# Row maxima of an attention unit: a 32x32 transpose on VectorE, or a transfer in four-byte pieces

## The chip, the cores and the metric

The kernel runs on one core of a Trainium2 chip. Its engines are named as in the profile: PE (TensorE, matmuls; PEld is its weight load), DVE (VectorE), ACT (ScalarE), POOL (GpSimd) and SP (SyncE, which here only issues DMAs). Each works through its own instructions in order and waits for others at semaphores. The metric is the device time of one execution in microseconds (us), the median of several runs.

## The reference

The input `x` has 2048 rows of 512. A scalar gate per row mixes an attention with 32 heads of size 16, which share one key and one value head, and a gated feed-forward layer. All is in float32.

```python
g = sigmoid((x * gate_w).sum(-1, keepdims=True))
q = (x @ wq).reshape(1, 2048, 32, 16).transpose(0, 2, 1, 3)
k, v = x @ wk, x @ wv
p = softmax(einsum("bhqd,bkd->bhqk", q, k) * 16 ** -0.5)
a = einsum("bhqk,bkd->bhqd", p, v).transpose(0, 2, 1, 3).reshape(1, 2048, 512) @ wo
b = ((x @ w_gate) * (x @ w_up)) @ w_down
out = g * a + (1 - g) * b
```

## The kernel before

The attention is cut into 64 units. A unit is 128 query rows of one group of 8 heads; `Q[u]` holds its queries transposed, four heads in each half of the partitions (0 to 63, 64 to 127). A softmax needs the maximum of each row of scores before the exponentials, so each unit is gone through twice.

The first pass (`p1`) makes scores with queries along the partitions: 32 matmuls a unit (L760), each 128 queries by 512 keys, and DVE takes the maximum of each (L761) into `mx`. After the 32nd, `p1_end` makes the unit's final maxima, 128 queries by 8 heads. The second pass (`p2`) makes the scores again, now with keys along the partitions: 32 matmuls (L801), each with an `Exp` on ACT (L802). The negated maximum enters these matmuls as two more rows of `Q`, rows 48 and 49 of each half: a high part in the format float32r, and a low part that holds what the rounding lost. So a unit's second pass can't begin before its two rows are in `Q`. After that `pv` sums the weighted values (L814), and `o_chain` normalises: a store of the sums, loads of them and of the denominators (`raw`, `dn`), sum (L658, L660) on POOL, reciprocals on DVE, a store of these (`dr`, L671), a load that spreads them (`rb`, L675), and a product on POOL (L679).

In `m` a query lies on a partition; in `Q`'s rows the queries lie along the row. Between them stands a transposition. Before the change it is DVE's: L769 takes the last maximum, L772 transposes blocks of 32x32, L773 negates and rounds, and L775 takes the low part. Four small DMAs then store the rows in DRAM (`dm`), one for each block, and two load them into `Q` (L788), one for each half.

Between these matmuls PE works on the feed-forward layer and the projections (L959). All of it is written out by a planner in the kernel: strings of letters set the order of the matmuls, and functions given to `later` are called when a modelled clock comes to them. `spend("dve", 800.0)` tells the planner that DVE is busy for 800 ns. The store is set 300 ns behind that, the fetch 3200 ns behind the store, and `mat[u]` tells when the second pass may start. These times only set places in the order; on the chip semaphores hold each instruction until what it needs is there. The first pass runs some 25 steps ahead of the second (`LEAD`).

All DMAs named here are issued by SP, in the planner's order. An instruction that waits there holds all DMAs behind it. POOL makes in the same way, in order, the splits of weights and hidden values into high and low parts (L142, L143), the products of the feed-forward layer (L581) and sums (L395).

Of the kernel before, what the change touches and what calls it, by code (L numbers as in the profile page):

```python
# [14 lines left out]
F32 = mybir.dt.float32  # L15
F32R = mybir.dt.float32r
AF = mybir.ActivationFunctionType
OP = mybir.AluOpType
AX = mybir.AxisListType
# [54 lines left out]
def mix_kernel(ctx: ExitStack, tc: tile.TileContext, x, wq, wk, wv, wo, wg, wu, wd, gw, out):  # L74
    nc = tc.nc
    PSUM = bass.MemoryType.PSUM
    consts = ctx.enter_context(tc.tile_pool(name="consts", bufs=1))
    work = ctx.enter_context(tc.tile_pool(name="work", bufs=2))
# [30 lines left out]
    z = consts.tile([128, NC * NT], F32, name="z")  # L109
    gg = consts.tile([128, NC * NT], F32, name="gg")  # L110
    gb = consts.tile([128, NC * NT], F32, name="gb")
    mm = [consts.tile([128, 32], F32, name=f"mm{i}") for i in range(2)]
    for t in mm:
        nc.gpsimd.memset(t, 0.0)
    woh = consts.tile([128, 4, D], F32R, name="woh")
    wol = consts.tile([128, 4, D], F32R, name="wol")

# [8 lines left out]
    def later(ns, fn):  # L126
        heapq.heappush(events, (clock["T"] + ns, next(serial), fn))
# [5 lines left out]
    def spend(eng, ns, after=0.0):  # L133
        clock[eng] = max(clock[eng], clock["T"], after) + ns
        return clock[eng]
# [26 lines left out]
    def bank(i, name):  # L162
        return psum.tile([128, 512], F32, name=name, tag=f"bank{i}")

    def ms_bank(i):
        return bank(i, f"ms{i}")
# [582 lines left out]
    mx, mat = {}, {}  # L749

    def p1(k, half, b):
        u, slot, kq = order1[k]
        c, g, t = units[u]
        q = Q[u]
        if u not in mx:
            mx[u] = work.tile([128, 8, 4], F32, name="mx", bufs=2)
            left[u] = 32
        p = bank(b, "s1")
        r = KROWS[half]
        nc.tensor.matmul(p, q[r, slot], KK[r, kq * 512:(kq + 1) * 512], start=True, stop=True)  # L760
        nc.vector.tensor_reduce(mx[u][:, half * 4 + slot, kq:kq + 1], p, axis=AX.X, op=OP.max)  # L761
        left[u] -= 1
        if left[u] == 0:
            p1_end(u)

    def p1_end(u):
        q = Q[u]
        m = mm[u % 2]
        nc.vector.tensor_reduce(m[:, 0:8], mx.pop(u), axis=AX.X, op=OP.max)  # L769
        w = work.tile([128, 3, 32], F32R, name="mt", bufs=2)  # L770
        mt = w[:, 0].bitcast(F32)
        nc.vector.transpose(mt, m)  # L772
        nc.vector.tensor_reduce(w[:, 1], mt.rearrange("p (q v) -> p q v", v=1), axis=AX.X, op=OP.max, negate=True)  # L773
        with nc.allow_low_precision(reason="the low part of two that are kept"):
            nc.vector.tensor_reduce(w[:, 2], w[:, 0:2].bitcast(F32).rearrange("p v q -> p q v"), axis=AX.X, op=OP.add)  # L775
        end = spend("dve", 800.0)
        d = dram.tile([2, 8, 128], F32, name="dm", tag="dm", bufs=2)

        def store():
            for b in range(4):  # L780
                nc.sync.dma_start(d[:, :, b * 32:b * 32 + 32].rearrange("v c q -> c v q"),
                                  w[b * 32:b * 32 + 8, 1:3].bitcast(F32))
            later(3200, fetch)

        def fetch():
            for half in range(2):
                r = half * 64 + 48
                nc.sync.dma_start(q[r:r + 2].bitcast(F32), d[:, half * 4:half * 4 + 4, :])  # L788
            mat[u] = clock["T"] + 4000.0
        later(end - clock["T"] + 300.0, store)  # L790
# [32 lines left out]
    p = bank(6, "warm")  # L823
# [3 lines left out]
    p = bank(6, "gwb")  # L827
# [8 lines left out]
    p = ms_bank(1)  # L836
# [21 lines left out]
    p = ms_bank(0)  # L858
# [234 lines left out]
    while events or front or st["gen"] or st["next"]:  # L1093
        run_events()
        if peek():
            j = take()
            items = j.prods()
            p = j.p
            if p is None:
                p = ms_bank(turn)  # L1100
# [24 lines left out]
```

## Time and profile before

| | |
|---|---|
| three timed runs | 1587.06, 1587.61, 1587.9 us |
| span of the profiled execution | 1586.4 us |
| what lies around the span (median less span) | 1.2 us |
| busy: PE, DVE, ACT, POOL | 1581.4, 1364.3, 1202.5, 732.5 us |
| L761, maxima of the first pass, 2048 times | 685 ns each, 1290.4 us |
| L772, L773, L775, 64 times each | median 211, 186, 222 ns |
| DMA packets, bytes | 184995, 121.20 MB |

The page gives a span and no other time of the profiled execution, so the third row takes the runs' median. Rows of the views read: line of the kernel, engine, operation, output and inputs by the program's names. Rows of a timeline begin with the start and the length in us, several equal instructions merged (x4). Rows of waits give the total in us, how often, and the longest. Rows of windows give the busy time of PE, PEld, DVE, ACT and POOL with the count of instructions in brackets, the granted clock of PE, the share of the DMA engines and GB/s; for one line alone, PE and PEld only.

### The profile page before, as it was taken

The page shows a single profiled execution, that of the slowest core. Times are in us where ns is not written, and L with a number is a line of the kernel's source. Part 1 is how long each engine was busy: PE and PEld are TensorE (multiplying, and loading weights), DVE is VectorE, ACT ScalarE, POOL GpSimd, SP SyncE. Part 2 cuts the span into 40 slices and gives each one's busy share as a digit, 9 for nine tenths or more (in the row PEclk, how much of TensorE's full clock was granted, in tenths as well). Part 3 has the DMA queues.
Part 4 walks back from the last instruction along what each step waited for, and adds up shares of the span by engine and source line. Part 5 has one row for each costly group of instructions (what it writes and reads, how often), then busy time and mean ns, then how long its engine had stood idle before and what let it go on. Part 6 is the DMA issues. An engine that isn't in the chain of part 4 may idle for free.

```text
span 1586.4 us, 35431 instructions
## 1 busy us (share of the span) xinstructions
PE 1581.4 (100%) x13144; PEld 1034.1 (65%) x13144; DVE 1364.3 (86%) x2411; ACT 1202.5 (76%) x2384; POOL 732.5 (46%) x871
## 2 busy tenths in 40 slices
PE   9999999999999999999999999999999999999999
PEld 7775666675665666675665666666666666676675
DVE  6998889898898889898898889898988989898982
ACT  5787787777787787777787787877787786877776
POOL 7535736253633624454532725444442615555340
PEclk9999999999999999999999999999999999999999
DMA  6554322122232212131232212122132212212111
GB/s 196 190 175 119 94 62 74 42 71 57 67 103 79 73 49 74 42 87 54 60 103 72 74 55 74 49 69 65 54 117 65 74 55 74 62 55 59 36 32 42
DMA packets 184995, 121.20 MB, mean 76 GB/s; under 512 B 46198, under 2 KB 154614, under 8 KB 184823
## 3 DMA queue, kind: packets, MB, share of 16 engines
q1 hardware_dynamic: 183620, 118.61, 25.1%
q8 instruction: 104, 1.70, 0.5%
q14 instruction: 69, 0.56, 0.1%
q10 hardware_dynamic: 1202, 0.33, 0.1%
HBM read 82.70 MB, written 36.17 MB: 75 GB/s over the span
## 4 chain that ended last, share of the span: by engine, by line
PE 99%; DVE 1%; issue 0%; POOL 0%; POOLq 0%
PE ms L959 32%; PE acc L814 29%; PE s L760 18%; PE s L801 17%; PE ms L155 1%; PE ms L1049 1%; DVE mx L761 0%; PE px L283 0%; PE wo L155 0%; PE warm L825 0%; PE px L270 0%; PE pv L325 0%; PE pick L725 0%; PE gwb L828 0%; DVE y L736 0%
## 5 line engine op out<-in xcount | busy, mean ns | idle before, releaser
L761 DVE TENSOR_REDUCE mx<-s 128x1 f32<-128x512 f32 x2048 | 1290.4, 685 | 170.0 <-PE s L760 107.7
L802 ACT ACTIVATE P<-s 128x512 f32<-128x512 f32 x2048 | 1056.1, 629 | 259.1 <-PE s L801 207.3
L760 PE MATMUL s<-KK,Q 48*128 48x512 f32 x2048 | 703.3, 401 | 0.2
L801 PE MATMUL s<-Q,KK 50*128 50x512 f32 x2048 | 701.9, 407 | 0.0
L814 PE MATMUL acc<-P,V 128*32 128x512 f32 x4096 | 478.8, 597 | 0.0
L801 PEld LDWEIGHTS s<-Q,KK 50*128 50x128 f32 x2048 | 355.5, 185 | 124.5 <-ACT P L802 47.6
L760 PEld LDWEIGHTS s<-KK,Q 48*128 48x128 f32 x2048 | 355.8, 185 | 101.7 <-issue 51.9
L959 PE MATMUL ms<-xh,wl 64*128 64x512 f32 x896 | 318.1, 392 | 0.0
L959 PE MATMUL ms<-xh,wh 64*128 64x512 f32 x896 | 313.6, 394 | 0.0
L959 PE MATMUL ms<-xl,wh 64*128 64x512 f32 x896 | 302.7, 391 | 0.0
L814 PEld LDWEIGHTS acc<-P,V 128*32 128x32 f32 x4096 | 117.9, 109 | 255.2 <-issue 221.0
L581 POOL TENSOR_TENSOR hf<-gs 128x512 f32<-128x512 f32 x56 | 72.1, 1287 | 216.3 <-ACT gs L570 216.3
L959 PEld LDWEIGHTS ms<-xh,wh 64*128 64x128 f32 x896 | 160.2, 186 | 14.6 <-issue 0.8
L959 PEld LDWEIGHTS ms<-xh,wl 64*128 64x128 f32 x896 | 159.3, 186 | 9.1
L959 PE MATMUL ms<-wdh,hl 64*128 64x512 f32 x448 | 162.1, 393 | 0.0
L679 POOL TENSOR_TENSOR oT<-raw,rb 128x128 f32<-128x128 f32 x63 | 29.0, 460 | 285.4 <-DMA rb<-dr 285.3
L959 PE MATMUL ms<-wdh,hh 64*128 64x512 f32 x448 | 160.3, 392 | 0.0
L959 PEld LDWEIGHTS ms<-xl,wh 64*128 64x128 f32 x896 | 152.2, 186 | 10.6
L395 POOL TENSOR_TENSOR y<-y,yt 128x512 f32<-128x512 f32 x58 | 74.7, 1288 | 171.8 <-ACT yt L394 163.6
L143 POOL TENSOR_TENSOR wl<-wn,wh 128x512 fp32r<-128x512 f32 x116 | 149.2, 1286 | 9.3
L959 PE MATMUL ms<-wdl,hh 64*128 64x512 f32 x448 | 153.3, 392 | 0.0
L818 ACT COPY osb<-acc 128x512 f32<-128x512 f32 x64 | 37.5, 587 | 95.3 <-PE acc L814 88.9
(179 smaller groups left out, 1375.5 us busy)
## 6 DMA issues: line engine op xcount, KB each, us to landing
do<-osb SPq DMA_DIRECT2D x63, 256.0 KB
wn<-in_B_w_gate_dram SPq DMA_DIRECT2D x56, 256.0 KB
wn<-in_B_w_up_dram SPq DMA_DIRECT2D x56, 256.0 KB
wdn<-in_B_w_down_dram SPq DMA_DIRECT2D x56, 256.0 KB
Q<-dq SPq DMA_DIRECT2D x384, 32.0 KB
raw<-do SPq DMA_DIRECT2D x252, 32.0 KB
dq<-oh SPq DMA_DIRECT2D x16, 256.0 KB
dq<-ol SPq DMA_DIRECT2D x16, 256.0 KB
```

The source lines that it names most:

```text
L143: nc.gpsimd.tensor_tensor(lo, src, hi.bitcast(F32), op=OP.subtract)
L155: nc.tensor.matmul(p, l, r, start=start and i == 0, stop=stop and i == len(prods) - 1)
L395: nc.gpsimd.tensor_tensor(y[c, t], y[c, t], tmp, op=OP.add)
L581: nc.gpsimd.tensor_tensor(hf, gu[0], gu[1], op=OP.mult)
L679: nc.gpsimd.tensor_tensor(dst, raw[:, 0], rb, op=OP.mult)
L760: nc.tensor.matmul(p, q[r, slot], KK[r, kq * 512:(kq + 1) * 512], start=True, stop=True)
L761: nc.vector.tensor_reduce(mx[u][:, half * 4 + slot, kq:kq + 1], p, axis=AX.X, op=OP.max)
L801: nc.tensor.matmul(p, KK[r, j * 128:(j + 1) * 128], q[r].rearrange("p s q -> p (s q)"), start=True, stop=True)
L802: nc.scalar.activation(P[s][:, half], p, AF.Exp, scale=0.25)
L814: nc.tensor.matmul(acc[u][b:b + 32, :], V[:, j + i], src[:, half], start=(j == 0), stop=(j == NJ - 2))
L818: nc.scalar.copy(osb, acc.pop(u))
L959: nc.tensor.matmul(j.p, lhs[HALVES[l]], rhs[HALVES[l]], start=(l == 0 and i == 0), stop=(l == 1 and end))
```

## The change

DVE keeps the last maximum (now L767), without the padding to 32 columns. POOL negates and rounds it (`tensor_scalar`, L768) and takes the low part (`tensor_tensor`, L769). Nothing is transposed on an engine: one DMA (L774) writes each of the 2048 numbers to its place in the rows in DRAM, in pieces of four bytes. The fetch is as before. Lines behind the change move up, by 2 to 8.

```diff
-    mm = [consts.tile([128, 32], F32, name=f"mm{i}") for i in range(2)]
-    for t in mm:
-        nc.gpsimd.memset(t, 0.0)
...
     def p1_end(u):
         q = Q[u]
-        m = mm[u % 2]
-        nc.vector.tensor_reduce(m[:, 0:8], mx.pop(u), axis=AX.X, op=OP.max)
-        w = work.tile([128, 3, 32], F32R, name="mt", bufs=2)
-        mt = w[:, 0].bitcast(F32)
-        nc.vector.transpose(mt, m)
-        nc.vector.tensor_reduce(w[:, 1], mt.rearrange("p (q v) -> p q v", v=1), axis=AX.X, op=OP.max, negate=True)
-        with nc.allow_low_precision(reason="the low part of two that are kept"):
-            nc.vector.tensor_reduce(w[:, 2], w[:, 0:2].bitcast(F32).rearrange("p v q -> p q v"), axis=AX.X, op=OP.add)
-        end = spend("dve", 800.0)
+        m = work.tile([128, 8], F32, name="m1", bufs=2)
+        w = work.tile([128, 2, 8], F32R, name="mw", bufs=2)
+        nc.vector.tensor_reduce(m, mx.pop(u), axis=AX.X, op=OP.max)
+        nc.gpsimd.tensor_scalar(w[:, 0], m, -1.0, None, op0=OP.mult)
+        nc.gpsimd.tensor_tensor(w[:, 1], m, w[:, 0].bitcast(F32), op=OP.add)
+        end = spend("pool", 450.0, spend("dve", 260.0) + 100.0)
         d = dram.tile([2, 8, 128], F32, name="dm", tag="dm", bufs=2)
 
         def store():
-            for b in range(4):
-                nc.sync.dma_start(d[:, :, b * 32:b * 32 + 32].rearrange("v c q -> c v q"),
-                                  w[b * 32:b * 32 + 8, 1:3].bitcast(F32))
+            nc.sync.dma_start(d.rearrange("v c q -> q (v c)"), w.bitcast(F32).rearrange("q v c -> q (v c)"))
             later(3200, fetch)
```

The new `spend` also moves the store and the fetch among SP's DMAs, and the two operations take a place among POOL's. The matmuls' and ACT's order stays as it is, but for some 80 places of PE in the first stage.

POOL at the end of unit 12, before the change (`den`, `raw`: sums of `o_chain`; `wh`, `wl`, `wdh`, `wdl`: parts of the weights; `hf`, `hh`, `hl`: the hidden values):

```order
L143 TENSOR_TENSOR wl<-wn,wh 128x512
L658 TENSOR_TENSOR den<-dn 128x8
L660 TENSOR_TENSOR raw<-raw 128x128
L142 CAST wdh<-wdn 128x512
L143 TENSOR_TENSOR wdl<-wdn,wdh 128x512
```

The same place now:

```order
L140 TENSOR_TENSOR wl<-wn,wh 128x512
L655 TENSOR_TENSOR den<-dn 128x8
L657 TENSOR_TENSOR raw<-raw 128x128
L768 TENSOR_SCALAR mw<-m_5425 128x8
L769 TENSOR_TENSOR mw<-m_5425,mw 128x8
L139 CAST wdh<-wdn 128x512
L140 TENSOR_TENSOR wdl<-wdn,wdh 128x512
```

The pair stands behind `raw`, and the splits of the next weights behind the pair.

SP at unit 1, before (`xd`: a store of transposed input for later; `dq`: queries in DRAM; `woh`, `wdl` stand here for parts of that input):

```order
L230 DMA Q<-dq 16x4x128 x6
L781 DMA dm<-mt 8x2x32 x4
L334 DMA xd_526<-wdl 128x512
L214 DMA dq<-oh 128x512
L214 DMA dq<-ol 128x512
L334 DMA xd_527<-woh 128x512
L788 DMA Q<-dm 2x512 x2
```

And now:

```order
L227 DMA Q<-dq 16x4x128 x6
L331 DMA xd_522<-wdl 128x512
L774 DMA dm<-mw 128x16x1
L331 DMA xd_523<-woh 128x512
L211 DMA dq<-oh 128x512
L211 DMA dq<-ol 128x512
L780 DMA Q<-dm 2x512 x2
```

The store of the maxima has gone behind one `xd` store; between it and the fetch stand three DMAs, where there were four.

## The prediction

> **What bounds the kernel now.** I read the page first (engines, chain), then the stages by windows, then the waits of TensorE, then the rows around one unit's end on each engine that the change touches. From the page, busy time by engine and the chain that ended last:
>
> ```profile
> span 1586.4 us, 35431 instructions
> PE 1581.4 (100%) x13144; PEld 1034.1 (65%) x13144; DVE 1364.3 (86%) x2411; ACT 1202.5 (76%) x2384; POOL 732.5 (46%) x871
> PE 99%; DVE 1%; issue 0%; POOL 0%; POOLq 0%
> ```
>
> A busy PE is not yet a PE that loses nothing, so two windows of 10 us, one early and one in the middle, and all that the waits list for PE's matmuls, and for its weight loads on the transposed maxima:
>
> ```profile
> core 0: us, PE busy (x) PEld busy (x) DVE busy (x) ACT busy (x) POOL busy (x), PEclk, DMA share, GB/s
> 50.00:60.00 10.00, 10.00 (x68) 8.34 (x68) 9.88 (x18) 6.62 (x15) 5.40 (x5) 1.00 0.72 257
> 700.00:710.00 10.00, 10.00 (x88) 7.93 (x84) 9.69 (x16) 8.76 (x18) 4.21 (x5) 1.00 0.35 99
> ...
> PE warm L825 <- POOL ident masks.py:199: 1.4, 1, 1.4
> ...
> PEld s L760 <- DVE mt L773: 6.7, 8, 0.8
> ```
>
> PE waits once, before its first matmul. The eight weight loads released by the maxima's reduces run ahead of matmuls that did not wait, so their 6.7 us are no gain to be had. In the middle of the run 88 matmuls go in 10 us at full clock; PE's own stream is the bound there, and DVE, at 9.69 of 10, keeps up. Only early on, at 50 to 60 us, with 68 matmuls and DVE at 9.88, does DVE set the pace. So less work on DVE can gain almost nothing, while anything that makes PE wait costs its full length. The question is whether a unit's maxima still arrive in time.
>
> **What is taken from DVE.** The end of the thirteenth unit (counted from 0, unit 12) on DVE:
>
> ```profile
> 334.18 0.18 DVE L769 TENSOR_REDUCE mm<-mx 128x8 f32<-128x32 f32 x1
> 334.40 0.21 DVE L772 STREAM_TRANSPOSE mt<-mm 128x32 f32<-128x32 f32 x1
> 334.65 0.19 DVE L773 TENSOR_REDUCE mt<-mt 128x32 fp32r<-128x32 f32 x1
> 334.87 0.22 DVE L775 TENSOR_REDUCE mt<-mt 128x32 fp32r<-128x64 f32 x1
> 335.01 2.47 DVE L761 TENSOR_REDUCE mx<-s 128x1 f32<-128x512 f32 x4
> ```
>
> L769 stays. The three behind it go: 0.21 + 0.19 + 0.22 = 0.62 us, 40 us of DVE over 64 units. All of that lies beside a PE that does not wait, so it is worth nothing, but for the first unit's end at 47 us, in the stretch where DVE sets the pace: at most 0.6 us, which I take. The two memsets of `mm` lie in the start, on POOL, ahead of nothing that is waited for: nothing.
>
> **The path of the maxima.** From the end of L769 to the first matmul that reads the result: DVE's rest, four stores, the landing, two fetches, their landing, L801. SP's rows for unit 12, and the count of L801 up to two times (384 is twelve units of 32, so unit 12 starts between them):
>
> ```profile
> 335.12 1.29 SPq L781 DMA_DIRECT2D dm<-mt  x4
> 336.51 0.41 SPq L181 DMA_DIRECT2D wn<-in_B_w_up_dram  x1
> 337.41 0.54 SPq L788 DMA_DIRECT2D Q<-dm  x2
> ...
> 0.00:343.70 343.70, 132.85 (x384) 66.53 (x384) 1.00 0.37 116
> 0.00:343.80 343.80, 132.85 (x385) 66.53 (x385) 1.00 0.37 116
> ```
>
> L769 ends at 334.36 and PE wants the rows at 343.75: 9.4 us. Today the first store follows 0.8 us behind L769, and 2.3 us later the fetch can go; issued by 337.95, it has some 5 us.
>
> **POOL's part.** Two operations on 128x8, priced by the nearest row, the sum of denominators L658 on the same shape, 0.20 us each; with two hand-overs I take 0.5 us from the moment POOL is free. POOL works in order, though. Its rows when L769 ends; the new pair stands behind `raw` and ahead of the cast of `wdh`:
>
> ```profile
> 335.10 1.27 POOL L143 TENSOR_TENSOR wl<-wn,wh 128x512 fp32r<-128x512 f32 x1
> 336.33 0.20 POOL L658 TENSOR_TENSOR den<-dn 128x8 f32<-128x8 f32 x1
> 336.49 0.45 POOL L660 TENSOR_TENSOR raw<-raw 128x128 f32<-128x128 f32 x1
> 336.89 0.61 POOL L142 CAST wdh<-wdn 128x512 fp32r<-128x512 f32 x1
> ```
>
> So POOL comes to the pair at 336.94, 2.6 us after L769. Unit 46 is like it: L769 on DVE, `raw` on POOL, and PE's start of the unit (1472 are 46 units of 32):
>
> ```profile
> 1143.92 0.19 DVE L769 TENSOR_REDUCE mm<-mx 128x8 f32<-128x32 f32 x1
> ...
> 1146.26 0.46 POOL L660 TENSOR_TENSOR raw<-raw 128x128 f32<-128x128 f32 x1
> ...
> 0.00:1153.60 1153.60, 507.10 (x1473) 256.04 (x1473) 1.00 0.28 82
> ```
>
> The same reading at all units, by the place of the pair in the new order: POOL is there within 0.4 us, or waits for L769 itself, in about half; 1.3 to 1.6 us late in about a dozen; 2.6 us late in ten, unit 12 to unit 46; over 3 us late in six, four of which have 11.3 us instead of 9.4. Where POOL comes early, the pair now holds the work behind it until L769 has ended, 5 us at most. That work feeds PE, but the matmuls' only wait names POOL before the start, and a POOL that is busy 46% makes it up: nothing.
>
> **The new store.** One DMA in place of four saves 0.9 us of SP's time and issues 2048 pieces of four bytes, over all 16 DMA engines, in place of 64 of 128 bytes. The nearest row is the store of the reciprocals, 128 pieces of 32 bytes from 128 partitions to DRAM. SP's issue and the load that waits for its landing, then the stretch in which its pieces move, then one on a load of the same count of pieces (`dn`) that goes over two engines only, then the queue's totals:
>
> ```profile
> 626.18 0.35 SPq L671 DMA_DIRECT2D dr<-rc  x1
> 626.57 0.43 SPq L181 DMA_DIRECT2D wn<-in_B_w_gate_dram  x1
> 627.60 0.61 SPq L675 DMA_DIRECT2D rb<-dr  x1
> ...
> 627.00:627.20 0.20, 0.20 (x4) 0.16 (x4) 0.00 (x0) 0.00 (x0) 0.00 (x0) 1.00 0.38 21
> 325.80:326.40 0.60, 0.60 (x8) 0.53 (x6) 0.60 (x1) 0.60 (x2) 0.52 (x2) 1.00 0.11 7
> ...
> q1 hardware_dynamic: 183620, 118.61, 25.1%
> ```
>
> Issue to landing is 1.42 us with 128 pieces, and these move at 21 GB/s, 1.5 ns a piece over all engines. 1920 pieces more at that pace are 3.0 us: landing after 4.4 us. The low end is the other load: 128 pieces in 0.6 us on two engines are 9.4 ns a piece on one engine, and 120 more on each would add 1.1 us: 2.5 us. The high end is the mean packet of the queue, 25.1% of 16 x 1586.4 us over 183620 packets, 34.7 ns: 120 of them add 4.2 us: 5.6 us. I take 4.4, since the row is a store to DRAM spread like the new one, and keep 2.5 and 5.6 for the range. No row has a piece of four bytes, so more than 5.6 isn't excluded either.
>
> The Trainium skill has a rule that speaks against this store: "DMA: Bandwidth & Descriptors", section Bandwidth, gives a floor of about 10.5 ns a packet for small transfers, measured on loads. The row above, at 1.5 ns a piece, does not agree, if the rule is meant for a whole transfer; by it the pieces alone would be an estimated 21.5 us.
>
> **The sum for one unit.** Unit 12: pair done 337.45, store lands 341.85, the fetch, a small DMA like the one that took 1.42 us, lands by 343.3; wanted at 343.75. On time by 0.45 us, where today it has some 4. Unit 46, the last of that class, reads the same (pair 1147.2, landing 1151.6, fetch 1153.0, wanted by 1153.6). Where POOL is free, the pair is done 0.6 us behind L769 and the margin is near 3 us. What is late at 4.4 us stands in the first units, where POOL and SP are in arrears. Unit 1 on SP, where the new store goes behind the `xd` store that now follows it, and the count of L801 (32 is one unit):
>
> ```profile
> 72.03 3.65 SPq L230 DMA_DIRECT2D Q<-dq  x6
> 75.78 1.38 SPq L781 DMA_DIRECT2D dm<-mt  x4
> 77.21 0.34 SPq L334 DMA_DIRECT2D xd<-wdl  x1
> ...
> 0.00:81.40 81.40, 11.02 (x32) 5.46 (x32) 1.00 0.58 196
> 0.00:81.60 81.60, 11.09 (x33) 5.56 (x33) 1.00 0.58 197
> ```
>
> SP is free at 75.7, stores `xd` for 0.35, issues at 76.1; landing 80.5, fetch in at 81.9, wanted at 81.5: 0.4 us late. In unit 0 POOL is the one: its L769 ends at 47.1, but the pair stands behind this multiplication, and PE wants the rows at 56.3:
>
> ```profile
> 49.08 1.29 POOL L342 TENSOR_TENSOR yt<-P,wdn 128x512 f32<-128x512 f32 x1
> ...
> 0.00:56.20 56.20, 0.00 (x0) 0.00 (x0) 1.00 0.53 174
> 0.00:56.40 56.40, 0.08 (x1) 0.08 (x1) 1.00 0.53 174
> ```
>
> Pair done 50.9, landing 55.3, fetch in at 56.7: 0.4 us late. Units 3 and 6 are late by 0.2 and 0.6, read in the same way. Together 1.6 us, and I take 2.0, since DMA is 72% busy in the window shown of that stage; all of it PE waiting. Sum: 1586.4 + 2.0 - 0.6 = 1587.8 us of span. The three timed runs have a median of 1587.61, 1.2 us above this span, so 1589.0 us as it is timed.
>
> SP waits with the fetch for the landing, up to 2 us longer than now, and loads behind the store find 128 pieces ahead of them on each engine. What is late next is the row of reciprocals `rb` and POOL's product with it:
>
> ```profile
> POOL oT L679 <- DMA rb<-dr: 285.3, 53, 12.3
> ```
>
> POOL already idles there for 5.4 us at a time without PE waiting; nothing, as long as it stays at 3 us more.
>
> **Rivals.**
>
> Slow pieces (the other side). Four bytes in DRAM may cost more than 32, and PE then waits for the bias rows. It decides from a landing of about 4.6 us: the ten units like unit 12 are then late together, and every further 0.1 us costs 1 us. At 5.6 us the same reading of all units finds 33 late by 24 us in all: 1611. At 7.2 us, 60 are late, mostly by 1 to 2.5 us: 96 us, 1683. Beyond that each microsecond costs 64. For it speaks that no row shows such a piece; against it that the 32-byte row needs so little.
>
> Cheap pieces: at the low end of 2.5 us no unit is late, and the first unit's 0.6 us remain: 1587. It can't be told from the forecast in the result, only in the profile.
>
> DVE's relief frees PE. If DVE held PE by more than the waits show, 64 x 0.62 us could come back in part; at a tenth, 4 us: 1583. The 88 matmuls a window and the lack of waits speak against it.
>
> A floor for each piece of the whole transfer. If pieces go one behind another at 10.5 ns, landing is 18.5 us later than in my sum, and less the margins of 0.4 to 3 us each unit is late by some 16.5 us: 64 x 16.5 = 1056, near 2640 us. The skill's floor, named above, is the reason to give it a chance at all.
>
> **How the numbers follow.** The timing can tell about 0.2% here, 3.2 us. A landing under 4.6 us, forecast and cheap pieces together: 0.50, all of it within 0.2% but for a little. Slow pieces: 0.42, of it 0.15 up to 1611 and 0.15 between there and 1670. DVE's relief: 0.05. The floor: 0.03. So faster 0.05, same 0.50, slower 0.45. The range leaves out the relief beyond 1585.5 and what lies above 1670; the likeliest case's own is 1586.5 to 1591.
>
> **What would show it.** In the changed profile: L772 to L775 gone and DVE at about 1325 us; POOL about 26 us busier; packets near 312,000, since 131,072 come and 4,096 go; from the new store's issue to the fetch some 4.4 us where the fetch stands right behind it; no wait of PE or PEld for a DMA on Q outside the first units. Wrong would be windows with fewer than 88 matmuls in the middle and a gap ahead of L801 once a unit: then the store is slower than I hold it to be.

## The result, and the profile after

The changed kernel takes 2027.11 us (median of four runs, 2023.06 to 2029.74), against 1587.63 us before. The ratio is 1.276, with a 95% interval of 1.2747 to 1.2777. The forecast was 1589.0 us, and the time lies far above its range of 1585.5 to 1670. Two single executions below, one of 5459.73 us with POOL's part alone and one of 3132.42 us with pieces of 64 bytes, lie far from all others at a full clock, and the ratios are made without them. The profiled execution has a span of 2028.0 us, 441.6 us more than before.

From the page after: busy times, the clock in 40 slices, packets, and the chain that ended last, by engine and by line.

```profile
span 2028.0 us, 35160 instructions
PE 1738.5 (86%) x13144; PEld 1199.9 (59%) x13144; DVE 1340.8 (66%) x2219; ACT 1240.1 (61%) x2384; POOL 757.7 (37%) x997
PEclk9888888998988989998988989988989889889889
DMA packets 310944, 121.18 MB, mean 60 GB/s; under 512 B 172149, under 2 KB 280565, under 8 KB 310774
DMA 40%; PE 39%; POOL 8%; issue 4%; ACT 4%; DVE 3%; SPq 2%; POOLq 0%; ACTq 0%; DVEq 0%
```

PE was 99% of the chain, and is now 39%; DMA has come from nothing to 40%. PE has the same 13144 matmuls as before, but its busy time has grown by 1738.5 - 1581.4 = 157.1 us, and its idle time by (2028.0 - 1738.5) - (1586.4 - 1581.4) = 284.5 us. These two are the whole loss. The list of PE's waits says what the idle time is:

```profile
PE s L793 <- DMA Q<-dm: 283.7, 65, 7.6
PE warm L817 <- POOL ident masks.py:199: 1.3, 1, 1.3
```

L793 is the matmul of the second pass's scores (L801 before): 65 waits, 4.4 us each, for the rows of maxima. One unit on SP: L774 is the new store, L780 the fetch, which SP can't issue before the store has landed.

```profile
425.79 0.38 SPq L774 DMA_DIRECT2D dm<-mw  x1
428.77 0.34 SPq L668 DMA_DIRECT2D dr<-rc  x1
436.32 0.56 SPq L780 DMA_DIRECT2D Q<-dm  x2
436.97 0.40 SPq L178 DMA_DIRECT2D wn<-in_B_w_gate_dram  x1
437.46 0.61 SPq L672 DMA_DIRECT2D rb<-dr  x1
```

SP stands ahead of the fetch in every unit, 536.7 us in all:

```profile
SPq L780 <- DMA dm<-mw: 536.7, 64, 10.6
```

From the issue of the store to its landing pass 10.53 us here; the mean over the 64 units is 10.8, and none is under 9.6. The fetch then takes 1.55 us to PE's matmul:

```profile
437.87 1.01 PE L793 MATMUL s<-Q,KK 50*128 50x512 f32 x2 [5.28 <-DMA Q<-dm]
```

The slow store also holds up the one behind it. In the unit shown `dr`, in pieces of 32 bytes, is issued 3.0 us later and lands 8.2 us behind its own issue, by the trace's completion marks; the mean is 7.4 us over the 55 stores whose marks are complete, against 1.8 us in the kernel before.

What the DMA engines and PE do meanwhile, in windows (columns as before: PE, PEld, DVE, ACT, POOL, granted clock, DMA share, GB/s):

```profile
426.70:428.30 1.60, 1.60 (x14) 0.64 (x18) 0.95 (x2) 1.13 (x3) 1.53 (x2) 1.00 0.74 51
428.30:429.40 1.10, 1.10 (x14) 0.20 (x6) 0.44 (x2) 0.93 (x2) 1.08 (x1) 1.00 0.00 0
429.40:429.90 0.50, 0.50 (x4) 0.42 (x6) 0.00 (x1) 0.04 (x1) 0.20 (x1) 1.00 0.15 8
429.90:436.30 6.40, 2.69 (x21) 0.69 (x17) 3.17 (x5) 1.65 (x3) 0.00 (x0) 1.00 0.00 0
436.90:444.00 7.10, 6.13 (x31) 6.16 (x33) 2.71 (x4) 3.79 (x7) 0.46 (x1) 0.55 0.39 123
444.00:446.00 2.00, 2.00 (x21) 1.68 (x18) 1.93 (x5) 1.94 (x5) 0.00 (x0) 1.00 0.13 21
```

The four-byte pieces pass through the DMA engines in the first row, and are through 2.5 us behind the issue. The third row is the store of `dr`, and in the 6.4 us behind it these engines move nothing at all, and the store of the maxima still hasn't landed. That is the first thing that the forecast had not seen: the landing isn't the time in which the pieces move. The second is in the fifth row. In the 7.1 us in which the rows come and the second pass sets in, PE's clock is 0.55. Half clock shows as 0.50, so (1 - 0.55) x 7.1 / 0.5 = 6.4 us of these are at half. With the mean clock of the whole run at 0.901, half clock holds 2028 x 0.099 / 0.5 = 401 us, 6.3 us a unit. In these stretches PE is busy for 290 us by the trace, at half speed, which is 145 us of work lost: most of the 157 us of longer matmuls.

### The profile page after: what moved, and what is told of

Its sections match the earlier page's. It is cut to its first block, busy times and chain, and to the rows that moved or that the text cites. A ratio compares the mean times of both kernels' runs of the same rounds, so it can differ in the third digit from the quotient of the medians.

```text
span 2028.0 us, 35160 instructions
## 1 busy us (share of the span) xinstructions
PE 1738.5 (86%) x13144; PEld 1199.9 (59%) x13144; DVE 1340.8 (66%) x2219; ACT 1240.1 (61%) x2384; POOL 757.7 (37%) x997
## 2 busy tenths in 40 slices
DMA packets 310944, 121.18 MB, mean 60 GB/s; under 512 B 172149, under 2 KB 280565, under 8 KB 310774
## 4 chain that ended last, share of the span: by engine, by line
DMA 40%; PE 39%; POOL 8%; issue 4%; ACT 4%; DVE 3%; SPq 2%; POOLq 0%; ACTq 0%; DVEq 0%
DMA dm<-mw 33%; PE ms L951 21%; PE s L793 10%; PE s L757 6%; DMA Q<-dm 5%; ACT P L794 3%; DVE mx L758 3%; SPq L227 1%; POOL hf L578 1%; DMA Q<-dq 1%; POOL hl L140 1%; PE ms L152 1%; ACT gs L567 1%; POOL mw L768 1%; POOL wl L140 1%
## 5 line engine op out<-in xcount | busy, mean ns | idle before, releaser
L794 ACT ACTIVATE P<-s 128x512 f32<-128x512 f32 x2048 | 1082.6, 612 | 658.9 <-PE s L793 496.4
L793 PE MATMUL s<-Q,KK 50*128 50x512 f32 x2048 | 772.3, 451 | 283.7 <-DMA Q<-dm 283.7
L757 PE MATMUL s<-KK,Q 48*128 48x512 f32 x2048 | 748.5, 426 | 0.5 <-ACT gs L367 0.2
L793 PEld LDWEIGHTS s<-Q,KK 50*128 50x128 f32 x2048 | 404.3, 210 | 417.8 <-issue 314.3
L757 PEld LDWEIGHTS s<-KK,Q 48*128 48x128 f32 x2048 | 387.4, 201 | 95.2 <-issue 52.0
L951 PE MATMUL ms<-xh,wl 64*128 64x512 f32 x896 | 347.1, 426 | 0.0
L951 PE MATMUL ms<-xh,wh 64*128 64x512 f32 x896 | 338.4, 431 | 0.0
L951 PE MATMUL ms<-xl,wh 64*128 64x512 f32 x896 | 329.8, 419 | 0.0
L676 POOL TENSOR_TENSOR oT<-raw,rb 128x128 f32<-128x128 f32 x63 | 28.8, 458 | 666.6 <-DMA rb<-dr 652.1
L951 PE MATMUL ms<-wdh,hh 64*128 64x512 f32 x448 | 180.7, 442 | 0.0
L951 PEld LDWEIGHTS ms<-xl,wh 64*128 64x128 f32 x896 | 172.5, 204 | 6.0
L810 ACT COPY osb<-acc 128x512 f32<-128x512 f32 x64 | 37.5, 586 | 97.6 <-PE acc L806 97.6
```

The costliest lines, as they stand in the source:

```text
L676: nc.gpsimd.tensor_tensor(dst, raw[:, 0], rb, op=OP.mult)
L793: nc.tensor.matmul(p, KK[r, j * 128:(j + 1) * 128], q[r].rearrange("p s q -> p (s q)"), start=True, stop=True)
L794: nc.scalar.activation(P[s][:, half], p, AF.Exp, scale=0.25)
L810: nc.scalar.copy(osb, acc.pop(u))
L951: nc.tensor.matmul(j.p, lhs[HALVES[l]], rhs[HALVES[l]], start=(l == 0 and i == 0), stop=(l == 1 and end))
```

## The experiments

Each is told by its edit against the kernel named. The time of the kernel before, measured beside them, is 1587.74 us for the first four and 1588.07 us for the last three. Behind each ratio stands its 95% interval. The two kernels with extra transfers ran once each (1612.42 and 1625.9 us), and only landings are read from them.

**POOL's part alone.** Against the kernel before: the transpose and the four stores stay, and only L773 and L775 go to POOL.

```diff
-        nc.vector.tensor_reduce(w[:, 1], mt.rearrange("p (q v) -> p q v", v=1), axis=AX.X, op=OP.max, negate=True)
...
-            nc.vector.tensor_reduce(w[:, 2], w[:, 0:2].bitcast(F32).rearrange("p v q -> p q v"), axis=AX.X, op=OP.add)
-        end = spend("dve", 800.0)
+        nc.gpsimd.tensor_scalar(w[:, 1], mt, -1.0, None, op0=OP.mult)
+        nc.gpsimd.tensor_tensor(w[:, 2], mt, w[:, 1].bitcast(F32), op=OP.add)
+        end = spend("pool", 450.0, spend("dve", 460.0) + 100.0)
```

> The kernel before, with POOL's part of the change alone: DVE keeps the transpose, POOL makes sign and split from the transposed rows (two operations on 128x32), the four stores of 128-byte pieces stay. Theory (the loss comes from the landing of the four-byte store): POOL's part costs at most 2 us, so 1586 to 1590 us, with no wait of PE for the rows of maxima after the first units. Rival (POOL's order makes the rows late, by 2.6 us and more at a third of the units): PE waits for them at those units, 1600 us or more.

Measured: 1589.92 us, ratio 1.0012 (1.0002 to 1.0022). PE waits for the rows twice, for 0.6 us together:

```profile
PE s L800 <- DMA Q<-dm: 0.6, 2, 0.4
```

Another 1.2 us of this execution are a wait for an input ahead of the first unit. So POOL's place in the order costs some 2 us, 0.3 to 3.5 by the interval, while the store lands as early as before, and the 440 us are the transfer's.

**PE kept busy while it waits.** Against the changed kernel: 20 matmuls without use stand ahead of each unit's first matmul of the second pass, into the same bank.

```diff
+        if j == 0 and half == 0:
+            for _ in range(20):
+                nc.tensor.matmul(p, KK[:, 0:128], KK[:, 0:512], start=True, stop=True)
```

> The changed kernel, with 20 more matmuls of 128x128 by 128x512 on PE ahead of the first matmul of each unit's second pass, into the bank which that matmul then overwrites; they wait for nothing that is late, and at 0.23 us each fill some 4.6 us of PE's wait for the rows. Theory (PE idles 284 us, and the other 157 us of the loss are PE at half clock for some 7 us behind each wait): the clock stays near 1.00, the wait for the rows is as long from store to landing as before, and the time falls by 100 to 157 us in spite of 1280 more matmuls: 1870 to 1930 us. Rival (the clock has no part in it; the rest of the loss is other engines late behind the wait): 2020 to 2060 us.

Measured: 1978.18 us, ratio 1.2464 (1.2445 to 1.2482): 49 us faster than the change, between the two expectations. The groups of PE's matmuls, L794 being the new ones (busy, mean ns, then the idle time ahead of them):

```profile
L757 PE MATMUL s<-KK,Q 48*128 48x512 f32 x2048 | 709.8, 404 | 0.4 <-ACT gs L367 0.2
L796 PE MATMUL s<-Q,KK 50*128 50x512 f32 x2048 | 702.3, 412 | 45.8 <-DMA Q<-dm 45.6
L794 PE MATMUL s<-KK 128*128 128x512 f32 x1280 | 311.3, 398 | 0.3 <-DVE mx L758 0.3
```

In the changed kernel L757 and L793 took 426 and 451 ns; with the gap filled they are back at 404 and 412 (401 and 407 before the change), and the mean clock is at 0.994. So it is the idle time that brings the slow clock. A unit's period, from the start of the second pass in unit 0 to that in unit 63, tells what it was worth: 30.65 us after the change, 6.85 above the 23.80 of before, of which 4.39 are idle time of PE and 2.46 the rest. Here it is 29.77, 5.97 above: 4.71 for the 20 matmuls (0.236 us each), 0.70 idle, 0.56 rest. The rest fell by 1.9 us, some 120 us in all. Not all of that came back, because the waiting part became longer: 20 matmuls are more than the wait in some units, and the landing took 11.3 us in the mean, against 10.8 after the change; why it did is open. It is 11.2 us in the unit shown (SP):

```profile
422.74 0.38 SPq L774 DMA_DIRECT2D dm<-mw  x1
433.93 0.56 SPq L780 DMA_DIRECT2D Q<-dm  x2
```

**Which transfer lands late.** The kernel before, with one extra transfer at every second unit, of eleven kinds in turn, and behind each one on SP a small transfer that waits for its landing.

```diff
+    def probe(kind, u):
...
+        nc.sync.dma_start(dst, src)
+        sink = dram.tile(list(back.shape), F32, name="ps", tag=f"ps{kind}", bufs=1)
+        nc.sync.dma_start(sink, back)
```

> The kernel before, with a transfer of its own at every second unit's end, which nothing uses: eleven kinds in turn, each followed on SP by a small load or store of what it wrote, so that SP's next issue shows the landing. All from 128 partitions: four-byte pieces to DRAM in rows of 128 as in the change, 2048, 1024 and 512 of them; the same 8 KB in 1024 pieces of 8 bytes, 512 of 16, 256 of 32, 128 of 64; 2048 pieces of 32 bytes; 2048 pieces of four bytes, each to the start of a 64-byte line of its own; 2048 of four bytes from SBUF to SBUF; 2048 of four bytes read from DRAM into SBUF. Theory A (DRAM is slow at writes shorter than its own unit): 2048 of four bytes 10.7 us, 1024 about 6, 512 about 3.7; 8 bytes about 6, 16 bytes 3.7; 32 and 64 bytes under 2; 2048 of 32 bytes under 5 in spite of the same count; own lines no faster than 9; SBUF to SBUF and reads from DRAM under 5. Theory B (it is the count of pieces written to DRAM): 2048 of 32 bytes 10 us as well. Theory C (neighbours' pieces share a line and wait for each other): own lines under 5. Theory D (it is the count of pieces anywhere): SBUF to SBUF 10 us as well.

SP's rows of five kinds, the extra transfer L816 and the one behind it, L818. In this order: 2048 pieces of four bytes packed in rows as in the change, 512 such pieces, 2048 pieces of 32 bytes, 2048 pieces of four bytes from SBUF to SBUF, and 2048 reads of four bytes from DRAM.

```profile
613.17 0.47 SPq L816 DMA_DIRECT2D pa<-ident  x1
624.04 0.57 SPq L818 DMA_DIRECT2D ps<-pa  x1
...
174.16 0.43 SPq L816 DMA_DIRECT2D pa<-ident  x1
182.83 0.63 SPq L818 DMA_DIRECT2D ps<-pa  x1
...
415.10 0.47 SPq L816 DMA_DIRECT2D pb16x<-ident  x1
418.70 0.55 SPq L818 DMA_DIRECT2D ps<-pb16x  x1
...
511.98 0.71 SPq L816 DMA_DIRECT2D pr<-ident  x1
515.58 0.64 SPq L818 DMA_DIRECT2D ps<-pr  x1
...
564.90 0.38 SPq L816 DMA_DIRECT2D pr<-pi  x1
568.19 0.60 SPq L818 DMA_DIRECT2D ps<-pr  x1
```

The difference of the two starts is the landing. All kinds, two or three times each:

| kind | us to landing |
|---|---|
| 4 bytes, packed in DRAM, 2048 / 1024 / 512 pieces | 10.9, 10.9 / 10.5, 9.8 / 8.7, 9.0, 8.3 |
| same bytes in pieces of 8 / 16 / 32 / 64 bytes | 4.3 to 4.6 / 2.6 to 3.8 / 2.0 to 2.9 / 2.3 to 2.7 |
| 2048 pieces of 32 bytes | 3.1 to 3.6 |
| 2048 pieces of 4 bytes, each 64 bytes from the next | 4.9 to 5.4 |
| 2048 pieces of 4 bytes, SBUF to SBUF | 3.6, 3.7 |
| 2048 reads of 4 bytes, DRAM to SBUF | 3.0, 3.3 |

So it isn't the number of pieces: a quarter of them lands only 2 us earlier, and as many pieces of 32 bytes land in a third of the time. It isn't the size of a piece alone either, since four-byte pieces that lie apart land in half the time. It takes small pieces that lie side by side in DRAM. Theories A, B and D fall with that. C has the direction, though pieces each 64 bytes from the next took 4.9 to 5.4 us and not under 5.

**The same four-byte steps on the side of the read.** Against the changed kernel: the store writes 64 bytes of each partition as they lie, and four loads pick the numbers out.

```diff
-            nc.sync.dma_start(d.rearrange("v c q -> q (v c)"), w.bitcast(F32).rearrange("q v c -> q (v c)"))
+            nc.sync.dma_start(d, w.bitcast(F32))
...
+                for v in range(2):
+                    nc.sync.dma_start(q[r + v:r + v + 1].bitcast(F32),
+                                      d[:, v:v + 1, half * 4:half * 4 + 4].rearrange("q v c -> v c q"))
```

> The changed kernel with the pieces on the other side: POOL's pair is stored as it lies, 128 pieces of 64 bytes, and the transposition is made by the fetch, four loads of 512 four-byte pieces from DRAM into one row each. Theory A (short writes to DRAM are slow, short reads are not): store 1.4 us, four loads landed within 3 to 6 us; PE waits at most at the units where POOL is late, 1587 to 1610 us. Rival (four-byte pieces are slow in either direction): some 9 us for the loads, 1900 us or more.

Measured: 2053.13 us, ratio 1.2925 (1.2899 to 1.2951). SP in the same place of the program, the two matmuls of PE that wait there, one for each half of `Q`, and PE's waits in all:

```profile
423.86 0.34 SPq L774 DMA_DIRECT2D dm<-mw  x1
426.83 0.33 SPq L668 DMA_DIRECT2D dr<-rc  x1
427.25 5.43 SPq L781 DMA_DIRECT2D Q<-dm  x4
...
434.35 0.76 PE L795 MATMUL s<-Q,KK 50*128 50x512 f32 x1 [3.72 <-DMA Q<-dm]
437.86 0.76 PE L795 MATMUL s<-Q,KK 50*128 50x512 f32 x1 [2.75 <-DMA Q<-dm]
```

```profile
PE s L795 <- DMA Q<-dm: 297.8, 119, 5.3
```

The store is no longer late: the loads are issued right behind `dr`, 3.4 us after it. But now the loads are. SP needs 5.4 us to issue four of them, and they land 5.2 to 7.6 us behind their issue, though the 2048 reads of the experiment before landed in 3.3 us. Those went to many partitions; these go to one partition each, and from 432 to 434 us, when only these pieces move, the DMA share is 0.24, the time of some four of the 16 engines. That the few partitions are the cause was not tested by itself. So this kernel loses as much, and the number is the rival's, but it doesn't tell on which side the four bytes cost more. The table does.

**Pieces of eight bytes.** Against the changed kernel: high and low part lie side by side.

```diff
-        w = work.tile([128, 2, 8], F32R, name="mw", bufs=2)
+        w = work.tile([128, 8, 2], F32R, name="mw", bufs=2)
...
-            nc.sync.dma_start(d.rearrange("v c q -> q (v c)"), w.bitcast(F32).rearrange("q v c -> q (v c)"))
+            nc.sync.dma_start(d.rearrange("v c q -> (v c q)").rearrange("(c q v) -> q c v", c=8, v=2), w.bitcast(F32))
```

> The changed kernel, but its row maxima go out as 1024 pieces of eight bytes, the high and the low part of one maximum side by side, instead of 2048 pieces of four; the bytes, POOL's pair, the queue and the fetch are the same. What it leaves out: the rows come back with the two parts interleaved, so the maxima stand in the wrong order. In the probe run 1024 pieces of eight bytes landed 4.25, 4.56 and 4.44 us behind their issue, which is the landing that the prediction took (4.4). If the landing was the prediction's only wrong term, the rest of its sum now gives the time: 1589 us, between 1587 and 1595, with no wait of PE for the rows above a few us in all and PE's clock near full. If something else in the change costs time (POOL late by its order in classes, the loads and stores that queue behind the store, the fetch ahead of p2), the time stays above 1600 although the landing is short.

Measured: 1602.54 us, ratio 1.0086 (1.0066 to 1.0106). Some 425 us have come back with nothing changed but the length of the pieces (and the order of the numbers in the rows), so the landing was by far the largest wrong term. But the time is 13.5 us above what the prediction's sum gives, outside the 1587 to 1595 expected here, and just above the line that was drawn for "something else". The landing is 4.2 to 6.1 us, in the mean 4.8, not the 4.4 of the sum. PE's waits:

```profile
PE s L793 <- DMA Q<-dm: 4.6, 6, 1.3
PE warm L817 <- POOL ident masks.py:199: 1.3, 1, 1.3
PE s L793 <- DVE mx L758: 0.8, 1, 0.8
```

And the clock behind the waits of units 0 and 3, 0.42 and 1.31 us long:

```profile
57.50:61.50 4.00, 3.92 (x19) 3.64 (x21) 1.88 (x3) 2.65 (x5) 0.49 (x1) 0.57 0.68 225
136.00:140.00 4.00, 4.00 (x24) 4.00 (x23) 2.73 (x4) 3.08 (x7) 0.46 (x1) 0.57 0.51 152
```

Set against the kernel before, matmul by matmul, L793 is late by 1.8 us in unit 0, 3.3 at unit 1, 7.1 in unit 3, 8.7 at unit 6 (where the wait is the third line above, put down to DVE), 9.4 at unit 8, and then by single steps, the largest 0.4, 1.0 and 1.4 us at units 28, 32 and 47, 13.0 at unit 47, where it about stays. A clock of 0.57 over 4 us is half clock for 3.4 us, in which PE does 1.7 us of work less; twice that are 3.4 of the 13 us. PE's idle time grew by 6 us, from 5.0 to 11.0. The other 4 us are matmuls that took longer, and stay open.

The Trainium skill, "TensorE: Matmul & The Clock Gate", Part 1, says that the clock goes to half after an idle window of about 3.4 us and back after a busy one, and that the windows run freely. The 3.4 us of half clock agree. The length of the idle time doesn't: here waits of 0.42 and 1.31 us stand ahead of it, and not a gap of 3.4. Nor does each wait bring it: behind those of 1.06 us at unit 1 and 0.91 us at unit 47 the granted clock stays at 1.00.

**Pieces of 64 bytes.** Against the changed kernel: the store writes 64 bytes of each partition as they lie, and the fetch is as in the change.

```diff
-            nc.sync.dma_start(d.rearrange("v c q -> q (v c)"), w.bitcast(F32).rearrange("q v c -> q (v c)"))
+            nc.sync.dma_start(d.rearrange("v c q -> (v c q)").rearrange("(q e) -> q e", e=16), w.bitcast(F32).rearrange("q v c -> q (v c)"))
```

> The changed kernel with 128 pieces of 64 bytes stored as they lie, so that nothing is turned into rows (this is left out; the fetch reads the same bytes in one contiguous order). VectorE's transpose and copies are gone as in the change, POOL's pair is there, and the landing is about 2.3 us by the probe run. If PE's stream is the bound and VectorE's relief is worth at most 0.6 us, against up to 2 us for POOL's part, the time is 1586.5 to 1589.5. If VectorE's relief freed PE (the rival of the prediction), it is 1583 or less.

Measured: 1589.35 us, ratio 1.0006 (0.9997 to 1.0015). From its page and its waits:

```profile
PE 1581.7 (100%) x13144; PEld 1036.3 (65%) x13144; DVE 1323.8 (83%) x2219; ACT 1202.9 (76%) x2384; POOL 758.1 (48%) x997
```

```profile
PE s L793 <- DVE mx L758: 0.3, 1, 0.3
```

DVE has 40.5 us less to do than before and POOL 25.6 us more, and the time is that of before. With the four-byte pieces gone, and with them the turning into rows, the rest of the change does nothing to the time, in either direction.

**How close pieces must lie.** The kernel before with extra transfers as above, of four-byte pieces only: 2048 at five steps in DRAM, rows of 128 adjacent pieces, and one row of 128 at three steps.

> The kernel before with one extra transfer from SBUF to DRAM at every second unit, of eleven kinds in turn, each followed on its queue by a transfer that waits for its landing. Kinds: 2048 pieces of four bytes at steps of 8, 16, 32, 128 and 256 bytes in DRAM; one, two and sixteen rows of 128 adjacent pieces of four bytes; one row of 128 pieces at steps of 8, 16 and 64 bytes. Theory of the shared line: pieces that fall into the same 64 bytes are written one after the other, about half a us each, so already one row of 128 adjacent pieces lands in 8 us or more, a step of 8 bytes in 4 to 5.5, 16 bytes in 3 to 5, and from a step of 64 bytes on 128 pieces land in under 2.5 us and 2048 in 5 or less. Theory of the count: the landing goes with the number of pieces, so 128 pieces land in under 2.5 us however close they lie, 256 a little above, and 2048 in 5 or more at every step.

SP's rows of one row of 128 adjacent pieces, of one row of 128 at a step of 16 bytes, and of 2048 at a step of 8 bytes and of 256 (L808, and behind it L810):

```profile
325.46 0.47 SPq L808 DMA_DIRECT2D pn<-ident  x1
333.86 0.57 SPq L810 DMA_DIRECT2D ps<-pn  x1
...
519.80 0.46 SPq L808 DMA_DIRECT2D po<-ident  x1
522.21 0.55 SPq L810 DMA_DIRECT2D ps<-po  x1
...
612.39 0.47 SPq L808 DMA_DIRECT2D pa<-ident  x1
619.38 0.59 SPq L810 DMA_DIRECT2D ps<-pa  x1
...
810.63 0.46 SPq L808 DMA_DIRECT2D pa<-ident  x1
815.46 0.58 SPq L810 DMA_DIRECT2D ps<-pa  x1
```

| four-byte pieces | us to landing |
|---|---|
| 128 adjacent / 256 in two rows / 2048 in sixteen rows | 7.4 to 8.4 / 7.5 to 8.5 / 10.5 to 11.1 |
| 128 at a step of 8 / 16 / 64 bytes | 3.1 to 4.2 / 2.4, 2.7 / 2.4, 2.4 |
| 2048 at a step of 8 / 16 / 32 / 128 / 256 bytes | 7.0, 7.2 / 6.1, 6.2 / 4.6 to 5.7 / 4.6 to 4.9 / 4.2 to 5.1 |

128 adjacent pieces are 512 bytes in all, and take some 8 us; at a step of 16 bytes the same 128 take 2.5. The theory of the count falls. Of the theory of the shared line the direction holds, and its number for one row of 128 adjacent pieces nearly (8 us or more expected, 7.4 to 8.4 measured), but not its proportion: it expected 4 to 5.5 us at a step of 8 bytes and 3 to 5 at 16, and all but one of these five landed earlier. With 128 pieces, writes that fall together hinder each other more than in proportion to how many they are. What unit they share, and whether they wait in a queue or read and write it back each time, these runs don't tell; nor whether it matters that neighbours in DRAM always came from different partitions. That is left open.

## Why the prediction was wrong, step by step

- **PE's stream is the bound, and DVE's relief is worth at most 0.6 us.** Right. With pieces of 64 bytes DVE has 40 us less to do and the time is within 0.2% of before. The rival in which DVE's relief frees PE is out. DVE's busy time in the changed kernel is 1340.8 us, not the 1325 forecast; with pieces of 64 bytes it is 1323.8.
- **POOL's pair, 0.5 us, and its place in the order.** Right. L768 and L769 have medians of 231 and 201 ns in the changed kernel. POOL's busy time rose by 25.2 us (26 forecast). Taken alone POOL's part costs some 2 us, and that it holds the work behind it shows in no wait of PE.
- **The landing of the new store, 4.4 us, between 2.5 and 5.6 taken for the sum.** This is the step that failed: 10.8 us. The packets were right, 310944 against 312,000, and the pace at which they pass was no slower than taken, 2048 pieces within 1.6 us (0.8 ns each, against 1.5). What failed is that this pace was taken for the landing, from a row of 128 pieces of 32 bytes. For pieces of that size the sum would have done: 2048 of them land in 3.1 to 3.6 us. But even 128 pieces of four bytes, as many as in that row, land only after some 8 us when they are adjacent. The text named the hole ("more than 5.6 isn't excluded") and still made the range up to 1670 from a landing below 7.2.
- **A floor of 10.5 ns a packet for the whole transfer.** By the row of 426.7 to 428.3 the pieces pass in 1.6 us, so no such floor holds for the transfer as a whole. By the floor that the Trainium skill states ("DMA: Bandwidth & Descriptors", section Bandwidth), taken for the whole transfer, it would be an estimated 21.5 us. A rule that was not used comes nearer. The Trainium skill, "DMA: Bandwidth & Descriptors", section "Anatomy of one DMA — SWDGE (gpsimd) path", says of DMAs that GpSimd issues that most of a transfer's fixed 2 us is the write receipt, and that it is heaviest for HBM. Here, with a DMA that SP issues, the DMA engines had been still for 6.4 us when the landing came, so the trace agrees in kind and not in size.
- **Margins: units 0, 1, 3 and 6 late, 2.0 us together.** The places were right, the sum too small. With pieces of eight bytes the loss up to unit 6 stands in just these units, but is 8.7 us: their landings are 4.9 to 6.1, and in units 0 and 3 a wait under 1.5 us was followed by 3.4 us of half clock. The class like unit 12, which was to go late together at 4.6 us, mostly did not: only a few later units did, by some 4 us in all.
- **The rival of slow pieces.** This is what happened, with a chance of 0.42, of which 0.12 lie above 1670, and a price that falls short. Its 64 us for each us of landing above 7.2 gives 1683 + 3.6 x 64 = 1913 us for 10.8. The wait itself was 283.7 us where this rule has 326. What it lacks is the 157 us of slower matmuls behind the waits, which only the rows of the clock show.
- **Loads behind the store, and `rb`.** POOL's wait for `rb` grew from 285.3 to 652.1 us, 5.8 us a unit: SP issues `rb` behind the fetch, which waits for the slow store, and `dr` itself lands late. That is more than the 3 us that the text allowed for. No wait of PE's list has POOL as its cause but the first, before the work begins; but PE was itself held up by 4.4 us in each unit, so this doesn't show what the lateness would cost a PE that isn't.
- **What would show it wrong** did: a gap ahead of the second pass once a unit, and windows with fewer matmuls, such as this one in the middle of the changed kernel (88 in 10 us before, and still 88 between two gaps, from 700 to 710 us):

```profile
1100.00:1110.00 10.00, 6.73 (x51) 2.59 (x49) 4.47 (x7) 3.74 (x7) 0.75 (x1) 0.94 0.19 27
```

No version here beats the kernel before, and none that leaves PE's stream as it is could by much: PE is busy for 1581 of its 1586 us.

## What to carry to other kernels

When a result is waited for, price a store by its landing, which is from its issue to the instruction that waits for it, and take the price from a row with pieces of the same size that lie as close together; the rate at which the DMA engines pass the pieces tells only when they are idle again. Where a layout must be turned on the way to DRAM, a piece of eight bytes instead of four can be the difference between a nearly hidden and a visible transfer (1602 and 2027 us here, though the rows of the first stand in the wrong order). Pieces that don't lie side by side landed earlier too, but no whole kernel here was built with them. And a wait on PE can cost more than its length: look at the granted clock behind it.

## What was not expected of the hardware

- Writes of four bytes side by side in DRAM: 128 of them, 512 bytes in all, land in 7.4 to 8.4 us, against 2.4 at a step of 64 bytes; 2048 land in 10.5 to 11.1, against 4.2 to 5.1 at 256. In the unit shown of the changed kernel no DMA engine moves anything for the last 6.4 us of 10.53. A store of 32-byte pieces issued 3.0 us later landed late with it, 8.2 us behind its issue.
- Four-byte pieces themselves are not slow: 2048 of them land in 3.6 us from SBUF to SBUF and in 3.0 to 3.3 as reads from DRAM.
- Loads of 512 four-byte reads into one partition each: SP took 5.43 us to issue four, and they landed 5.2 to 7.6 us behind their issue.
- PE at half clock for 6.4 us around the end of a wait of 5.28 us, and for 3.4 us behind waits of 0.42 and 1.31 us, but not behind waits of 1.06 and 0.91 us in the same execution.
